# The closing rows of q's projection from VectorE's sums, q's modulated weights a tile later, and another order at the start

## The chip, the cores and the metric

The kernel runs on one core of one Trainium2 chip. The metric is the device time of one execution in microseconds (us), here the median of three runs. Beside it stands one execution recorded by the hardware profiler. The engines of the core are TensorE (PE; its weight loads are PEld), VectorE (DVE), ScalarE (ACT), GpSimd (POOL) and SyncE (SP, which only issues DMAs here). Each takes its instructions in the order of the program and waits for others through semaphores.

## What is computed

One block with adaptive layer norm (adaLN) over x of 2048 tokens by 448 channels, in fp32: a linear attention with 16 heads of 28 channels, then a token-mixing MLP with 1792 hidden units.

```python
mod = (silu(c) @ w_mod).reshape(1, 6, 1, 448)
sa, ca, ga, sb, cb, gb = [mod[:, i] for i in range(6)]
h = layernorm(x) * (1 + ca) + sa
x = x + ga * A(h, wqkv, wo)
h = layernorm(x) * (1 + cb) + sb
x = x + gb * B(h, w1, b1, w2, b2)

# A: q, k, v = split(h @ wqkv); phi(t) = where(t > 0, t + 1, exp(t)) + 1e-6
# kv = phi(k)^T v; z = sum over tokens of phi(k)
# o = phi(q) kv / (phi(q) . z + 1e-6); A = o @ wo
# B: transpose(gelu(w1^T h + b1) ...) over the token axis, @ w2 + b2
```

The first layer norm never appears as a tensor. With mean m and standard deviation s of a token, (LN(x) * (1 + ca) + sa) @ W equals (x @ W' - m * colsum(W') + s * (sa @ W)) / s, where W' is W with its rows scaled by 1 + ca. So x^T is multiplied by the modulated weight W', and two rows close the product: the negated column sums of W' (which meet the mean) and sa @ W (which meets the standard deviation). 1/s is applied as the scale of the activation that reads the result.

## The kernel before

All work is written out in program order by hand (`manual_schedule`): each engine executes its instructions in the order in which the code emits them. Tokens are worked in 16 tiles of 128. To keep fp32 precision with the faster fp32r matmuls, each operand is split into a rounded part ("high", made by a ScalarE copy) and the remainder ("low", a VectorE subtraction), and a product takes three matmuls: high by high, high by low, low by high. The 448 channels are four chunks: three of 128 and one of 64, whose upper half holds low parts.

**Buffers.** Most tiles come from a pool of 74 equal SBUF slots; PSUM is a pool of 8 banks of 128 by 512 (`bank`). A new tile waits until a buffer is free.

**Start (lines 88 to 219, 554 to 669).** Constants are made on POOL and VectorE, among them `mask` (a block diagonal of the heads, three POOL instructions; it is read only at line 806, after the kv loop) and the selectors `sel_f` and `sel_b`, whose columns 64, 66 and 96, and 65, 67 and 97, pick the closing rows. SP issues the loads. `col_sum(j, ch)` computes the columns 1 + ca (j = 1) and sa (j = 0) on VectorE. Index j of the weights is 0 for q, 1 for k, 2 for v. `w_high` (ScalarE) and `w_low` (VectorE) make the two parts of W'. `row_part(j, ch)` sums sa * W over the chunks on VectorE into `accb`. `row_sum(j)` multiplies the four high and three low parts by `sel_s` (seven fp32r matmuls); `row_bias(j)` adds the sums of `accb` by one fp32 matmul, which the profile shows as two steps. `row_out(j)` copies the rows out of PSUM (ScalarE) and makes their low part (VectorE) into `Wrow`. `close(t, j)` is the last matmul of each projection; it multiplies those rows by the transposed statistics of the tile.

**Statistics.** Tiles 0 and 1: `a_stats_act` on ScalarE, whose `end01` finishes on VectorE and POOL (`a_pow`, a power for standard deviation and its reciprocal). All others, in pairs: `a_stats_dve` on VectorE, with `first` (bn_stats), `second` (bn_aggr) and `end` (one VectorE step, then POOL's power). `a_rows(t)` spreads the statistics of a pair into a row tile, `a_transpose(t)` transposes it on TensorE into a bank, and `a_copy(t)`, `a_copy(t + 1)` bring it into the tiles' operands on ScalarE; `close` needs them.

**The kv loop (lines 672 to 762), t = 4 to 15.** In tile t TensorE gets, in this order: `project(t + 1, 1)` (ten matmuls of k), `close(t, 1)`, at t = 9 q's `row_sum(0)` and `row_bias(0)`, `a_outer(t - 4)` (eleven matmuls that add x^T phi(k) of tile t - 4 into the four `cacc` banks), at odd t a transpose of rows for tiles t + 1 and t + 2, from t = 10 one early projection of q (`a_q`, ten matmuls and a close), and at t = 12 `mod_sum2(2)`, one matmul into a bank that `mod_out(2)` empties. ScalarE gets the copies of rows, `a_exp` (exp and ReLU for phi(k), which free the bank of k's projection), the high parts for tile t + 3 (`a_split_high`), for phi(k) (`a_pk_parts`) and for the normed x of tile t - 2 (`a_high`), and at t = 4 to 7 `w_high(0, t - 4)`. VectorE gets the statistics of later tiles, `w_low` and `row_part` for q at t = 5 to 8, `a_norm`, `a_pk`, the low parts (`a_split_low`, `a_low`) and the sums of later modulations (`mod_part`). POOL issues accumulating DMAs (`pkl`, lines 521 and 535) and does the powers. `a_phi_q(keep)` runs exp, ReLU and phi on the q projections in PSUM but the last `keep`.

At t = 9 `a_exp(t, kp)` stands ahead of the two `a_copy`; at other tiles behind them. Q's early projections are those of tiles 0 to 4, at t = 10 to 14; the other eleven (`late`) follow behind the loop, where TensorE goes on with the last `a_outer`, kv, the output projection and the two matmuls of the MLP until the end.

Of the kernel before, what the change touches and what calls it, by code (L numbers as in the profile page):

```python
# [14 lines left out]
P = 128  # L15
# [9 lines left out]
PRE_LOAD = {14: 2, 15: 4}  # L25
KV_LAG = 4
HIGH_AT = {13: (11, 12), 14: (13,), 15: (14, 15)}
Q_EARLY = {10: 0, 11: 1, 12: 2, 13: 3, 14: 4}
RING = 3
FETCH = {4: 11, 5: 12, 7: 13, 9: 14, 10: 15}  # L30
SUM_DMA = range(2, 13)
# [21 lines left out]
def block_kernel(ctx: ExitStack, tc: tile.TileContext, x, xt, wqkv, wo, w1, b1, w2, b2, c, wmod, wfirst, out):  # L53
# [38 lines left out]
    ident = cst.tile([P, P], F32, name="ident")  # L92
    make_identity(nc, ident)
    mask = cst.tile([G, D], F32, name="mask")
    nc.gpsimd.memset(mask, 1.0)
    m3 = mask.rearrange("p (g h d) -> p g h d", g=4, d=DH)
    nc.gpsimd.affine_select(out=m3, in_=m3, compare_op=ALU.is_ge, fill=0.0, base=0,
                            pattern=[[0, 4], [-DH, 4], [0, DH]], channel_multiplier=1)
    nc.gpsimd.affine_select(out=m3, in_=m3, compare_op=ALU.is_ge, fill=0.0, base=DH - 1,
                            pattern=[[0, 4], [DH, 4], [0, DH]], channel_multiplier=-1)  # L100
# [10 lines left out]
    for i in (64, 66, 96):  # L111
        nc.gpsimd.memset(sel_f[:, i:i + 1], -1.0)
        nc.gpsimd.memset(sel_b[:, i + 1:i + 2], 1.0)
    sel_s = cst.tile([P, ROWS], F32R, name="sel_s")
    rowst = []
    for i in range(RING):
        rowst.append(cst.tile([P, P], F32R, name=f"rowst{i}"))
# [161 lines left out]
    def row_part(j, ch):  # L279
        if ch == 0:  # L280
            accb[j] = slot(f"accb{j}")
            nc.vector.tensor_scalar_mul(accb[j], raw_w[j, 0], col[0][:, 0:1])
        else:
            nc.vector.scalar_tensor_tensor(accb[j], raw_w[j, ch], col[0][:, ch:ch + 1], accb[j],
                                           op0=ALU.mult, op1=ALU.add)
# [6 lines left out]

    def row_bias(j):
        nc.tensor.matmul(rowb[j][:ROWS, :D], sel_b, accb.pop(j), start=False, stop=True)

    def row_out(j):
        ps, w = rowb.pop(j), Wrow[j]
# [284 lines left out]
    w_row(1)  # L582
    act01, end01 = a_stats_act((0, 1))
    act01(0)
    for ch in (0, 2):
        col_sum(0, ch)
        col_sum(0, ch + 1)
        row_part(1, ch)
        row_part(1, ch + 1)
    row_sum(1)  # L590
    act01(1)
    end01()
    a_split(3)
    projects(in_turn(3)[:4], 1, "kp")
    row_bias(1)
    projects(in_turn(3)[4:], 1, "kp")
    a_split_high(4)
    a_split_high(5)
    low = a_rows(0)
    first23, second23, end23 = a_stats_dve((2, 3))  # L600
    first23(0)
    low()
    first23(1)
    second23(0)
    second23(1)
    end23()
    row_out(1)
    a_split_low(4)
    a_transpose(0)
    a_copy(0)  # L610
    a_copy(1)
    a_norm(0)
    a_split_low(5)
    projects(in_turn(4)[:3], 1, "kp")
    kps = [close(t, 1) for t in (0, 1)]
    projects(in_turn(4)[3:], 1, "kp")
    load_xt(9)
    load_x(9)
    load_mod(2)
# [48 lines left out]
    sum_end()  # L668
    a_split(7)
    wo_sb = []  # L670
    late = [t for t in range(NT) if t not in Q_EARLY.values()]
    for t in range(4, NT):
        if 5 < t < NT - 1:
            project(t + 1, 1, "kp")
        kp = close(t, 1) if t > 4 else kps[4]
        if t == 9:
            row_sum(0)
            row_bias(0)
        if t > 4:
            a_outer(t - KV_LAG)  # L680
        if t % 2 and 4 < t < NT - 2:
            a_transpose(t + 1)
        if t in Q_EARLY:
            a_q(Q_EARLY[t])
        if t == 12:
            mp = mod_sum2(2)
        pair = t % 2 and 7 < t + 3 < NT
        if pair:
            first, second, end = a_stats_dve((t + 3, t + 4))
            first(0)  # L690
        if 5 <= t < 9:
            w_low(0, t - 5)
        if pair:
            second(0)
        if 5 <= t < 9:
            row_part(0, t - 5)
        a_phi_q(t in Q_EARLY)
        if t == 9:
            a_exp(t, kp)
        if t % 2 and 4 < t < NT - 2:  # L700
            a_copy(t + 1)
            a_copy(t + 2)
        if t != 9:
            a_exp(t, kp)
        if 7 < t + 3 < NT:
            a_split_high(t + 3)
        a_pk_parts(t - 1)
# [19 lines left out]
            second(1)  # L727
            end()
        sum_end()
        if 4 <= t < 8:  # L730
            w_high(0, t - 4)
            if t == 7:
                w_row(0)
        if t == 9:
            row_out(0)
        if t == 12:
            mod_out(2, mp)
        if t in FETCH:
            load_xt(FETCH[t])
            load_x(FETCH[t])  # L740
# [620 lines left out]
```

## Time and profile before

| | us |
|---|---|
| median of the three runs | 436.14 (436.09 to 436.59) |
| profiled execution, span | 434.3 |
| PE busy | 428.0 |
| DVE busy | 362.4 |
| ACT busy | 278.7 |
| POOL busy | 118.6 |

The views used below are: the chain of work that ended last (followed back from the last instruction, each step to what released it); windows (busy time of each engine in a stretch, with instruction counts, granted TensorE clock, DMA share and GB/s); and the timeline of one engine, where a row is start, duration, engine, line of the kernel, operation, output <- inputs, shapes and count, and in brackets the idle time before it with what ended it. Neighbours on VectorE and ScalarE overlap a little, so a step from start to start is shorter than the duration shown. Matmuls are pipelined: one of 448 columns shows 0.36 us but the next starts 0.20 us later.

### The profile page before, as it was taken

Reading aid. Unit: us, or ns where it says so; the run is one execution under the profiler, and the core shown is the slowest. Engines: PE = TensorE matmul, PEld = TensorE weight load, DVE = VectorE, ACT = ScalarE, POOL = GpSimd, SP = SyncE. Lnnn points to the kernel's source line nnn. Section 1 sums busy time; section 2 is a strip of 40 time slices with the busy share of each in tenths; the row PEclk is TensorE's granted clock in tenths of the full one; section 3 lists DMA queues with packets and bytes.
Section 4 is the critical chain, followed back from the end, with each engine's and each line's share of the span. In section 5 each row is a group of like instructions: output and inputs, shape, how many; then the busy total and the mean of one; then the engine's idle time right before and its main releaser. Section 6 shows DMA issues by size and latency. Waiting matters only on the chain.

```text
span 434.3 us, 7208 instructions
## 1 busy us (share of the span) xinstructions
PE 428.0 (99%) x2333; PEld 395.3 (91%) x2333; DVE 362.4 (83%) x813; ACT 278.7 (64%) x595; POOL 118.6 (27%) x198
## 2 busy tenths in 40 slices
PE   8999999999999999999999999999999999999996
PEld 7688899999799989989999999999999999999996
DVE  4899987689799999996679695739798998898893
ACT  5799868658568799985855273537464664645550
POOL 4335443200025477765200000010113131132010
PEclk9999999999999999999999999999999999999999
DMA  8998996564300036345427461587469987885430
GB/s 285 383 331 166 241 248 160 108 222 167 87 1 0 26 72 149 73 97 122 146 85 230 154 211 50 163 211 203 84 183 213 205 181 153 215 183 118 82 54 32
DMA packets 63941, 66.14 MB, mean 152 GB/s; under 512 B 4960, under 2 KB 55456, under 8 KB 63904
## 3 DMA queue, kind: packets, MB, share of 16 engines
q1 hardware_dynamic: 54832, 50.90, 37.5%
q0 software_dynamic: 8784, 14.32, 20.9%
q10 hardware_dynamic: 288, 0.46, 0.4%
q8 instruction: 18, 0.29, 0.3%
q14 instruction: 19, 0.16, 0.1%
HBM read 46.30 MB, written 7.34 MB: 124 GB/s over the span
## 4 chain that ended last, share of the span: by engine, by line
PE 92%; DVE 4%; DMA 2%; issue 1%; POOL 0%; ACT 0%; SPq 0%; DVEq 0%
PE y L1156 19%; PE up L935 10%; PE up L937 10%; PE up L936 10%; PE y L1157 9%; PE cacc L548 8%; PE qp L436 7%; PE op L878 6%; PE kp L436 5%; PE tq L848 1%; PE op L885 1%; DMA wr<-in_qkv_dram 1%; PE kp L443 1%; DMA xt<-in_xt_dram 1%; PE qp L443 1%; PE kvb L802 1%
## 5 line engine op out<-in xcount | busy, mean ns | idle before, releaser
L935 PE MATMUL up<-h2h,ph 128*128 128x448 f32 x224 | 81.3, 363 | 0.0
L937 PE MATMUL up<-h2h,pl 128*128 128x448 f32 x224 | 81.2, 362 | 0.0
L936 PE MATMUL up<-h2l,ph 128*128 128x448 f32 x224 | 80.8, 361 | 0.0
L1111 POOL DMA_DIRECT2D a<-a x16 | 14.1, 953 | 138.7 <-DMA a<-in_B_w_dram 77.5
L937 PEld LDWEIGHTS up<-h2h,pl 128*128 128x128 f32 x224 | 42.0, 188 | 3.2
L936 PEld LDWEIGHTS up<-h2l,ph 128*128 128x128 f32 x224 | 41.9, 187 | 3.2 <-DVE h2l L932 0.3
L935 PEld LDWEIGHTS up<-h2h,ph 128*128 128x128 f32 x224 | 42.0, 188 | 2.2
L85 DVE TENSOR_TENSOR pl<-pr,ph 128x512 fp32r<-128x512 f32 x46 | 30.8, 687 | 4.1 <-ACT ph L84 3.3
L1162 ACT ACTIVATE cc<-y 128x448 f32<-128x448 f32 x24 | 13.0, 545 | 26.9 <-PE y L1157 26.9
L84 ACT ACTIVATE ph<-pr 128x512 fp32r<-128x512 f32 x46 | 27.6, 622 | 0.8 <-PE up L937 0.5
L1075 DVE TENSOR_TENSOR u<-u,mod 128x448 f32<-128x448 f32 x14 | 8.7, 622 | 21.7 <-ACT u L1074 21.5
L1074 ACT ACTIVATE u<-up,b1c 128x448 f32<-128x448 f32 x14 | 8.7, 624 | 24.1 <-PE up L937 23.5
L436 PE MATMUL kp<-wh,hh 128*128 128x448 f32 x64 | 24.0, 380 | 0.0
L548 PE MATMUL cacc<-pkh,xh 128*128 128x448 f32 x64 | 23.6, 369 | 0.0
L1176 POOL DMA_DIRECT2D out_dram<-yt x14 | 12.7, 908 | 39.9 <-DVE yt L1167 30.6
L436 PE MATMUL qp<-wh,hh 128*128 128x448 f32 x64 | 23.4, 366 | 0.0
L828 POOL TENSOR_SCALAR den<-den 128x16 f32<-128x16 f32 x16 | 8.8, 548 | 45.3 <-DVE den L825 45.3
L548 PE MATMUL cacc<-pkl,xh 128*128 128x448 f32 x56 | 20.3, 362 | 0.0
L878 PE MATMUL op<-wph,pth 128*128 128x448 f32 x48 | 18.7, 389 | 0.0
L1117 DVE TENSOR_TENSOR a<-a,s 128x512 f32<-128x512 f32 (+1 forms) x32 | 18.5, 619 | 0.0
L84 ACT ACTIVATE s2h<-s 128x512 fp32r<-128x512 f32 (+1 forms) x16 | 8.3, 569 | 15.5 <-DVE s L1117 15.5
L1156 PE MATMUL y<-ub,a11h 128*128 128x448 f32 x56 | 18.2, 375 | 0.0
(239 smaller groups left out, 1376.4 us busy)
## 6 DMA issues: line engine op xcount, KB each, us to landing
pr<-in_B_w_dram SPq DMA_DIRECT2D x56, 256.0 KB, 3.0
a<-in_B_w_dram SPq DMA_DIRECT2D x32, 256.0 KB, 4.5
a<-in_B_w_dram SPq DMA_DIRECT2D x32, 192.0 KB, 4.5
xt<-in_xt_dram SPq DMA_DIRECT2D x16, 256.0 KB, 5.0
x<-in_A_x_dram SPq DMA_DIRECT2D x16, 224.0 KB, 5.0
wm<-in_B_wmod_dram SPq DMA_DIRECT2D x16, 196.0 KB, 5.0
out_dram<-x SPq DMA_DIRECT2D x14, 224.0 KB, 2.2
out_dram<-yt POOLq DMA_DIRECT2D x14, 224.0 KB, 5.4
```

The lines of the kernel that those rows point to most:

```text
L84: nc.scalar.activation(hi, full, AF.Copy)
L85: nc.vector.tensor_sub(lo, full, hi.bitcast(F32))
L436: nc.tensor.matmul(pps[t, j][:, :D], a[:, ch * P:(ch + 1) * P], w, start=first, stop=False)
L548: nc.tensor.matmul(cacc[ch][:, :D], a[:, s], b, start=(t == 0 and i == 0), stop=(t == NT - 1 and i == len(todo) - 1))
L878: nc.tensor.matmul(opb[t][:, :D], a, b, start=(ch == n == 0), stop=False)
L935: nc.tensor.matmul(ps[:, :D], hi[:, sl], mh, start=first, stop=False)
L936: nc.tensor.matmul(ps[:, :D], hi[:, sl], ml, start=False, stop=False)
L937: nc.tensor.matmul(ps[:, :D], lo[:, sl], mh, start=False, stop=last)
L1111: nc.gpsimd.dma_start(w, a, accum_op=ALU.add)
L1117: nc.vector.tensor_tensor(w, raw2[q, a][i], raw2[q, b][i], op=op)
L1156: nc.tensor.matmul(ps[:, :D], h[:, s], w, start=opens and r == 0, stop=False, skip_group_check=True)
L1157: nc.tensor.matmul(ps[:, :HD], l[:, s], wh, start=False, stop=closes and r == PAIRS - 1, skip_group_check=True)
```

## The change

Five edits. (1) The closing rows of q: VectorE sums (1 + ca) * W over the chunks (`row_main`, tiles 6 to 9) beside `row_part`'s sum; `row_fold` (tile 10) folds each 128-partition sum to 64 partitions in one tile, both sums together, and splits it into high and low; `row_both` (tile 11) multiplies them by a new selector `sel_q`, in two fp32r matmuls in place of seven and one. `sel_g` is filled by seven POOL memsets at the end of tile 7 and copied to `sel_q` on ScalarE. (2) `w_high`, `w_low` and `row_part` of q come a tile later. (3) Q's early projections move from tiles 10 to 14 to tiles 12 (two), 13, 14 and 15, and the special order at t = 9 goes. (4) At the start the statistics of tiles 0 and 1, their rows, the transpose, `row_out(1)` and the first two closes stand in another order. (5) `mask` is made at the end of tile 12.

```diff
-Q_EARLY = {10: 0, 11: 1, 12: 2, 13: 3, 14: 4}
+Q_EARLY = {12: (0, 1), 13: (2,), 14: (3,), 15: (4,)}
+ROW_AT, QPREP = 11, 5
...
-    nc.gpsimd.memset(mask, 1.0)
...
+    def make_mask():
+        nc.gpsimd.memset(mask, 1.0)
...
+    sel_g = cst.tile([P, ROWS], F32, name="sel_g")
+    sel_q = cst.tile([P, ROWS], F32R, name="sel_q")
...
+    accs = {}
+
+    def row_main(j, ch):
+        p = slice(0, P) if ch < 3 else slice(0, 64)
+        if ch == 0:
+            accs[j] = slot(f"accs{j}")
+            nc.vector.tensor_scalar_mul(accs[j], raw_w[j, 0], col[1][:, 0:1])
+        else:
+            nc.vector.scalar_tensor_tensor(accs[j][p], raw_w[j, ch][p], col[1][p, ch:ch + 1], accs[j][p],
+                                           op0=ALU.mult, op1=ALU.add)
+
+    def row_fold(j):
+        s, b = accs.pop(j), accb.pop(j)
+        nc.vector.tensor_add(s[:64], s[:64], s[64:])
+        nc.vector.tensor_add(s[64:], b[64:], b[:64])
+        hi, lo = moving(slot, f"rfh{j}"), moving(slot, f"rfl{j}")
+        nc.scalar.activation(hi, s, AF.Copy)
+        nc.vector.tensor_sub(lo, s, hi.bitcast(F32))
+        accs[j] = (hi, lo)
+
+    def row_both(j):
+        rowb[j] = bank(f"rowb{j}")
+        for i, m in enumerate(accs.pop(j)):
+            nc.tensor.matmul(rowb[j][:ROWS, :D], sel_q, m, start=(i == 0), stop=(i == 1))
...
     act01(0)
+    act01(1)
     for ch in (0, 2):
         col_sum(0, ch)
         col_sum(0, ch + 1)
+        if ch == 2:
+            end01()
         row_part(1, ch)
         row_part(1, ch + 1)
     row_sum(1)
-    act01(1)
-    end01()
+    a_rows(0)()
     a_split(3)
     projects(in_turn(3)[:4], 1, "kp")
     row_bias(1)
+    a_transpose(0)
     projects(in_turn(3)[4:], 1, "kp")
     a_split_high(4)
-    a_split_high(5)
-    low = a_rows(0)
     first23, second23, end23 = a_stats_dve((2, 3))
     first23(0)
-    low()
+    row_out(1)
+    a_copy(0)
+    a_copy(1)
+    a_split_high(5)
     first23(1)
     second23(0)
     second23(1)
     end23()
-    row_out(1)
+    kps = [close(t, 1) for t in (0, 1)]
     a_split_low(4)
-    a_transpose(0)
-    a_copy(0)
-    a_copy(1)
     a_norm(0)
     a_split_low(5)
-    projects(in_turn(4)[:3], 1, "kp")
-    kps = [close(t, 1) for t in (0, 1)]
-    projects(in_turn(4)[3:], 1, "kp")
+    projects(in_turn(4), 1, "kp")
...
-        if t == 9:
-            row_sum(0)
-            row_bias(0)
+        if t == ROW_AT:
+            row_both(0)
         if t > 4:
             a_outer(t - KV_LAG)
         if t % 2 and 4 < t < NT - 2:
             a_transpose(t + 1)
-        if t in Q_EARLY:
-            a_q(Q_EARLY[t])
+        for i in Q_EARLY.get(t, ()):
+            a_q(i)
...
-        if 5 <= t < 9:
-            w_low(0, t - 5)
+        if QPREP < t <= QPREP + 4:
+            w_low(0, t - QPREP - 1)
         if pair:
             second(0)
-        if 5 <= t < 9:
-            row_part(0, t - 5)
-        a_phi_q(t in Q_EARLY)
-        if t == 9:
-            a_exp(t, kp)
+        if QPREP < t <= QPREP + 4:
+            row_part(0, t - QPREP - 1)
+        if ROW_AT - 5 <= t < ROW_AT - 1:
+            row_main(0, t - ROW_AT + 5)
+        if t == ROW_AT - 1:
+            row_fold(0)
+        a_phi_q(len(Q_EARLY.get(t, ())))
         if t % 2 and 4 < t < NT - 2:
             a_copy(t + 1)
             a_copy(t + 2)
-        if t != 9:
-            a_exp(t, kp)
+        a_exp(t, kp)
...
-        if 4 <= t < 8:
-            w_high(0, t - 4)
-            if t == 7:
+        if QPREP <= t < QPREP + 4:
+            w_high(0, t - QPREP)
+            if t == QPREP + 3:
                 w_row(0)
-        if t == 9:
+        if t == 7:
+            nc.gpsimd.memset(sel_g, 0.0)
+            for i in (64, 66, 96):
+                nc.gpsimd.memset(sel_g[:64, i:i + 1], -1.0)
+                nc.gpsimd.memset(sel_g[64:, i + 1:i + 2], 1.0)
+            nc.scalar.activation(sel_q, sel_g, AF.Copy)
+        if t == ROW_AT:
             row_out(0)
         if t == 12:
             mod_out(2, mp)
+            make_mask()
```

More of the change, by code (lines that the diff above doesn't have):

```diff
@@ L94, in block_kernel @@
     mask = cst.tile([G, D], F32, name="mask")
[L95 to L100, printed above, removed]
+    def make_mask():
+        nc.gpsimd.memset(mask, 1.0)
+        m3 = mask.rearrange("p (g h d) -> p g h d", g=4, d=DH)
+        nc.gpsimd.affine_select(out=m3, in_=m3, compare_op=ALU.is_ge, fill=0.0, base=0,
+                                pattern=[[0, 4], [-DH, 4], [0, DH]], channel_multiplier=1)
+        nc.gpsimd.affine_select(out=m3, in_=m3, compare_op=ALU.is_ge, fill=0.0, base=DH - 1,
+                                pattern=[[0, 4], [DH, 4], [0, DH]], channel_multiplier=-1)
     cst.tile([P, 112], F32, name="space")
@@ L670, in block_kernel @@
     wo_sb = []
-    late = [t for t in range(NT) if t not in Q_EARLY.values()]
+    late = [t for t in range(NT) if t not in sum(Q_EARLY.values(), ())]
     for t in range(4, NT):
```

## The prediction

> **What bounds the kernel now.** I read first the chain of work that ended last, by engine, then the busy times of two stretches: tiles 4 to 9 of the kv loop (33 to 53.5 us) and its rest.
>
> ```profile
> PE 92%; DVE 4%; DMA 2%; issue 1%; POOL 0%; ACT 0%; SPq 0%; DVEq 0%
> ```
> ```profile
> 33.07:53.52 20.45, 20.45 (x100) 17.87 (x100) 20.05 (x51) 18.05 (x36) 11.43 (x12) 1.00 0.96 206
> 53.52:87.37 33.85, 33.85 (x170) 31.48 (x170) 25.35 (x60) 24.49 (x50) 11.48 (x12) 1.00 0.75 170
> ```
>
> The columns are the stretch, its length, then PE, PEld, DVE, ACT and POOL busy. TensorE bounds the whole: a matmul less is time gained, if nothing else then comes late. But in the first stretch VectorE is busy 20.05 of 20.45 us. It is a second bound there, with no room. After 53.5 us it has room (25.35 of 33.85), because TensorE is then given q's early projections (one a tile from tile 10). The profiled span is 434.3 us, 1.84 under the median of 436.14; I sum on the trace and add the result to the median.
>
> **The change part by part.**
>
> *The closing row of Wq on TensorE.* The chain has:
>
> ```profile
> 49.02 1.42 PE rowb L291 x7
> 50.44 0.75 PE rowb L294 x2
> ...
> 98.38 0.40 PE zp L781 x2
> ```
>
> Nine steps, 2.17 us, become two matmuls of the kind of L781, 0.40: **-1.8 us**.
>
> *The start.* Statistics of tiles 0 and 1 are finished earlier, and row_out(1) is moved ahead on VectorE.
>
> ```profile
> 15.22 0.19 ACT L344 ACTIVATION_READ_ACCUMULATOR junk<-x,as 128x1 f32 x1
> ...
> 15.51 1.39 DVE L284 SCALAR_TENSOR_TENSOR accb<-wr,col,accb 128x448 f32<-128x448 f32 x2
> 16.89 0.16 DVE L371 TENSOR_SCALAR ve<-as 128x4 f32<-128x4 f32 x1
> ...
> 17.13 1.41 POOL L356 TENSOR_TENSOR mv<-ve,roots 128x4 f32<-128x4 f32 x1 [3.76 <-DVE ve L371]
> ...
> 18.58 0.17 DVE L399 CAST rowst<-mv 128x8 fp32r<-128x8 f32 x1 [0.93 <-POOL mv L356]
> ...
> 20.33 0.63 DVE L299 TENSOR_TENSOR wrow<-rowb,wrow 2x448 fp32r<-2x448 f32 x1
> ...
> 21.11 0.65 PE L443 MATMUL kp<-wrow,hl 98*128 98x448 f32 x2 [0.76 <-DVE wrow L299]
> ```
>
> The sums of squares are there at 15.41, so `end01` can run between the two row pairs, at 15.51, instead of behind them near 16.9; POOL's power starts some 1.3 us earlier and VectorE's wait of 0.93 us shrinks to 0.2 or 0.3. TensorE's closing matmuls can start some 1.6 us earlier, but three matmuls that stood ahead of them now stand behind, and what follows waits for VectorE, which is nearly full from here on:
>
> ```profile
> 20.00:25.00 5.00, 4.24 (x21) 3.47 (x20) 4.87 (x13) 4.15 (x11) 1.01 (x1) 1.00 1.06 383
> ```
>
> So the gain is what VectorE's wait loses: **-0.7 us** on both engines.
>
> *The mask.* It leaves POOL's start, where the rows below give 1.91 us from its first step to `sel_b`; nobody waits for these. At tile 12 POOL is idle most of the time, and the mask is read only after the loop. Zero; with no such room it would delay the DMAs behind it by these 1.9 us.
>
> ```profile
> 1.32 0.47 POOL L95 MEMSET mask<- 112x448 f32 x1
> ...
> 3.23 0.20 POOL L108 MEMSET sel_b<- 128x98 f32 x1
> ```
>
> *What VectorE gets.* `row_main` is four more instructions of the kind of L282 and L284, `row_fold` two adds and a subtraction with a ScalarE copy in between, as in `halves` (L235, L240).
>
> ```profile
> 35.87 0.42 DVE L282 TENSOR_SCALAR accb<-wr,col 128x448 f32<-128x448 f32 x1
> ...
> 39.34 0.68 DVE L276 SCALAR_TENSOR_TENSOR wl<-wr,col,wh 128x448 fp32r<-128x448 f32 x1
> 39.94 0.68 DVE L284 SCALAR_TENSOR_TENSOR accb<-wr,col,accb 128x448 f32<-128x448 f32 x1
> ...
> 69.58 0.62 DVE L235 TENSOR_TENSOR acc<-acc 48x448 f32<-48x448 f32 x1
> 70.85 0.62 DVE L240 TENSOR_TENSOR mh<-acc,mh 64x448 fp32r<-64x448 f32 x1 [0.64 <-ACT mh L237]
> ```
>
> The long ones follow each other at 0.60 (39.34 to 39.94), overlapping by 0.08; the first row part takes 0.34 so reckoned. The fold costs 71.47 - 69.58 = 1.9 and another add of 0.54: 2.4 us. Together 0.34 + 3 x 0.60 + 2.4 = 4.5 us, all ahead of `row_both`, in the stretch where VectorE has 0.4 us free. `w_low` and `row_part` move from tiles 5 to 8 to tiles 6 to 9, so VectorE is 0.94 us ahead after tile 5, then pays +0.1, +0.6, +0.6 and +1.8 in tiles 6 to 9. [...]
>
> *A new wait on ScalarE.* The copy of `sel_g` into `sel_q` stands at the end of tile 7 in ScalarE's queue. It waits for POOL's memsets, which stand behind that tile's power and a DMA issue, and the power waits for VectorE's last statistics of the tile. Behind the copy stand exp(8) and all of tile 8, for which VectorE waits in turn.
>
> ```profile
> 47.69 0.17 DVE L390 TENSOR_SCALAR ve<-mv 128x4 f32<-128x4 f32 x1
> ...
> 48.25 0.69 DVE L276 SCALAR_TENSOR_TENSOR wh<-wr,col,wh 64x448 fp32r<-64x448 f32 x1
> ...
> 50.07 0.62 DVE L458 SCALAR_TENSOR_TENSOR pk<-ek,rk 128x448 f32<-128x448 f32 x1
> ...
> 51.28 0.22 DVE L505 TENSOR_TENSOR xh<-xn,xh 128x64 fp32r<-128x64 f32 x1
> ...
> 52.47 0.62 DVE L384 BATCH_NORM_STATS2 st<-x 128x6 f32<-128x448 f32 x1
> ```
> ```profile
> 47.95 1.17 POOL L356 TENSOR_TENSOR mv<-ve,roots 128x4 f32<-128x4 f32 x1 [0.67 <-DVE ve L390]
> 49.08 1.08 POOL L535 DMA_DIRECT2D pk<-pk  x1
> ```
> ```profile
> 3.87 0.29 ACT L556 ACTIVATE sel_s<-sel_f 128x98 fp32r<-128x98 f32 x1 [1.20 <-POOL sel_f L112]
> ...
> 47.49 0.62 ACT L450 ACTIVATE ek<-kp,mv 128x448 f32<-128x448 f32 x1
> ...
> 50.12 0.56 ACT L500 ACTIVATE xh<-xn 128x448 fp32r<-128x448 f32 x1
> ```
>
> VectorE's tile 8 starts at 48.25 now; in the new order at 48.25 - 0.7 - 0.94 + 0.1 + 0.6 = 47.3, and I take 47.8, half a microsecond for small waits (tile 9 has two, quoted below). The last statistics of tile 7 are then at 47.2, the power runs at 47.5 to 48.6, the DMA issue to 49.7, the seven memsets (the first 0.20 as L108, the others smaller) to 50.1, the copy (0.29 as L556) to 50.4, exp(8) and its ReLU, some 1.1, to 51.5. VectorE wants pk(8) at 47.8 + 1.82 + 0.60 = 50.2: it waits 1.4. The next, xh(6), ends 3.2 us behind exp(8)'s start (47.49 to 50.68), at 53.6, where VectorE comes at 51.6 + 1.2 = 52.8: it waits 0.85. Bounds of this part: zero, if POOL comes to the memsets early, and 2.25; I take **2.25**, since each link is in the rows. [...]
>
> *When `row_both` can run.* Tile 9 on VectorE now:
>
> ```profile
> 54.81 0.69 DVE L419 TENSOR_TENSOR hl<-xt,hh 128x512 fp32r<-128x512 f32 x1 [0.56 <-ACT hh L415]
> ...
> 56.36 0.23 DVE L505 TENSOR_TENSOR xh<-xn,xh 128x64 fp32r<-128x64 f32 x1 [0.32 <-ACT xh L500]
> ...
> 57.38 0.63 DVE L299 TENSOR_TENSOR wrow<-rowb,wrow 2x448 fp32r<-2x448 f32 x1
> ...
> 59.01 0.51 DVE L496 TENSOR_SCALAR xn<-x,mv 128x448 f32<-128x448 f32 x1
> ```
> ```profile
> 62.20 0.36 PE L548 MATMUL cacc<-pkh,xh 128*128 128x448 f32 x1
> ```
>
> Tile 9 starts at 47.8 + 4.22 + 0.60 + 2.25 = 54.9. It takes 6.54 now (52.47 to 59.01); without the two waits (1.0 with the lost overlaps) and row_out's 0.66 it is 4.85, with three added steps of 0.60 6.6: tile 10 starts at 61.5, the fold ends at 63.9, TensorE's `outer(7)` starts at **64.1**. `outer(7)` starts at 62.20 now, behind one q projection of eleven matmuls, 2.2 us at the 0.20 of L781's row. Without it, without the 2.2 of the row's nine steps and 0.7 earlier, TensorE would be at `row_both`, right ahead of `outer(7)`, at 57.1. It waits, first for hl(12) in tile 9 and then for the fold, and the new order still has that q projection ahead of it. So the net so far, with all gains of TensorE in it, is 64.1 + 2.2 - 62.2 = **+4.1 us**.
>
> *PSUM.* All eight banks count. At tile 11 the four `cacc`, kp11, kp12, `rowb` and the transposed rows are eight; kp13 needs the bank that the copies of the rows free. Now tile 9 frees kp9 early, by exp(9) ahead of the copies; that is taken out and not put at tile 11. At tile 13 the four `cacc`, kp13, q0, q1 and `modp` are eight, and kp14 waits for `mod_out(2)`.
>
> ```profile
> 53.25 0.27 PE L408 MATMUL rw<-ident,rowst 128*98 128x128 f32 x1
> ```
> ```profile
> 53.55 0.57 ACT L411 ACTIVATE hl<-rw 34x128 fp32r<-34x128 f32 x2 [1.82 <-PE rw L408]
> ...
> 74.87 0.52 ACT L201 ACTIVATE mod<-modp 128x448 f32<-128x448 f32 x1
> ```
>
> The first costs 53.25 to 54.12, some 0.85; the second 0.52 and a hand-over of 0.3 as between these rows, 0.8. From zero to 1.65; I take **1.6**, as the counts leave no ninth bank.
>
> *The rest.* Two q projections at tile 12 and one in each of 13 to 15 cost TensorE what they cost before. Buffers of q's tiles and of Wq are held about two tiles longer. SP's loads already wait for such buffers:
>
> ```profile
> SPq L138 <- DVE accb L284: 2.4, 1, 2.4
> ```
>
> They will land later, but have a tile or more in hand: zero; with that gone, a wait like this row's 2.4.
>
> Sum: +4.1 + 1.6 = **+5.7 us**: 440.0 on the trace, **441.8** beside the median.
>
> **The rivals.** (a) *Faster.* The added steps fall into room that VectorE finds; then only -1.8 and -0.7 stay: 433.6. For it: the two waits in tile 9. Against: they total 0.9 us in the rows, where 4.5 are added. The place is the end of the fold: if it comes before 58.2 on the trace (59.8 if no bank is short), the change gains, later it loses; I reckon 63.9. 13%. (b) *ScalarE's new wait costs nothing*: 2.25 less and 0.6 of the small waits, 439.0. 18%. (c) *A bank is free*: 440.2. 11%; (b) and (c) together 437.4, 5%. (d) *The clock falls while TensorE waits* about 2.4 us at `row_both`. The granted clock is 1.00 in the stretches above and TensorE's longest wait in these rows is 0.76, so none shows it. At half speed the 11 + 10 matmuls behind, of 0.2 each, would take 4.2 us more: 446.0. 4%. [...] (e) *Nothing*: the VectorE load is half of what I reckon and eats the gains, 436.1. 3%.
>
> **How the numbers follow.** The forecast has 46%, with 440.4 to 443.2 as its own range (the 0.5 of small waits, a power of 1.17 or 1.41, one bank wait less or smaller). Leaving out (a), (d) and (e) is 20%, so the range reaches from (b) with (c) to the forecast's upper end: 437.2 to 443.2. About 0.2%, 0.9 us, is what can be told from no change. Faster 13%; same 5%, (e) and some of (b) with (c); slower 82%.
>
> **What would show it.** Right: ScalarE idle some 4 us ahead of the copy to `sel_q`, released by POOL; VectorE waiting at pk(8); VectorE full from 34 to 64 us; TensorE waiting about 2 us or more at `row_both` for the fold; gaps of 0.8 ahead of kp13 and kp14; the start 0.7 earlier. Wrong: TensorE without gaps from 50 to 64 us, or a fold that ends before 60.

## The result, and the profile after

| | before | after |
|---|---|---|
| median of the timed runs, us | 436.12 (435.98 to 436.59) | 447.27 (446.91 to 447.74) |
| profiled execution, span | 434.3 | 445.2 |
| mean granted TensorE clock | 1.000 | 0.991 |
| TensorE's row matmul `zp` (the landmark ahead of the kv product) starts at | 98.21 | 107.96 |

The changed kernel takes 11.15 us more: a ratio of 1.0257 (1.0244 to 1.0269). 441.8 was forecast with a range up to 443.2, so the sign was right and the size was not. Of the 10.9 us between the two traces 9.8 are there when `zp` starts; the kv loop is the place.

The chain of work that ended last, after, by engine:

```profile
PE 83%; DVE 8%; ACT 3%; DMA 2%; POOL 1%; issue 1%; SPq 0%; DVEq 0%; ACTq 0%; POOLq 0%
```

TensorE had 92% of it before. The missing part went to VectorE, ScalarE and POOL. TensorE's own waits name the places (engine, line waited for: us in total, times, longest):

```profile
PE rw L439 <- DVE rowst L433: 4.2, 2, 4.0
PE rowb L325 <- ACT rfh L318: 2.2, 1, 2.2
PE warm L192 <- DVE roots L110: 1.1, 1, 1.1
PE kp L467 <- ACT hl L442: 0.7, 1, 0.7
PE kp L467 <- ACT mod L207: 0.6, 1, 0.6
```

The two largest are new: 4.0 us at a transpose of rows, 2.2 at `row_both`. The two of 0.7 and 0.6 stand ahead of the projections of tiles 13 and 14. The 4.0 is read backwards through three queues. First TensorE and VectorE:

```profile
50.04 0.37 PE L579 MATMUL cacc<-pkl,xh 128*128 128x448 f32 x1
54.42 0.32 PE L439 MATMUL rw<-ident,rowst 128*98 128x128 f32 x1 [4.02 <-DVE rowst L433]
```
```profile
50.42 0.17 DVE L430 CAST rowst<-mv 128x8 fp32r<-128x8 f32 x1 [0.50 <-POOL mv L387]
53.67 0.63 DVE L489 SCALAR_TENSOR_TENSOR pk<-ek,rk 128x448 f32<-128x448 f32 x1 [3.07 <-ACT rk L484]
54.21 0.16 DVE L433 TENSOR_TENSOR rowst<-mv,rowst 128x4 fp32r<-128x4 f32 x1
...
55.73 0.23 DVE L536 TENSOR_TENSOR xh<-xn,xh 128x64 fp32r<-128x64 f32 x1 [0.76 <-ACT xh L531]
```

The step that TensorE wants, L433, takes 0.16 us and its inputs had been there since 50.6. It stands behind phi(k) (L489) in VectorE's queue, and that waits 3.07 us for ScalarE's ReLU. Now ScalarE and POOL:

```profile
45.30 0.66 ACT L270 ACTIVATE wh<-wr,col 128x448 fp32r<-128x448 f32 x1
52.30 0.28 ACT L769 ACTIVATE sel_q<-sel_g 128x98 fp32r<-128x98 f32 x1 [6.35 <-POOL sel_g L768]
52.49 0.62 ACT L481 ACTIVATE ek<-kp,mv 128x448 f32<-128x448 f32 x1
53.01 0.62 ACT L484 ACTIVATE rk<-kp,mv 128x448 f32<-128x448 f32 x1
```
```profile
47.43 2.96 POOL L387 TENSOR_TENSOR mv<-ve,roots 128x4 f32<-128x4 f32 x1 [1.25 <-DVE ve L421]
50.36 0.91 POOL L566 DMA_DIRECT2D pk<-pk  x1
50.97 0.50 POOL L765 MEMSET sel_g<- 128x98 f32 x1
```

ScalarE stands idle for 6.35 us ahead of a copy of 0.28; some 2.2 of these it would have waited in any case, as k's projection of tile 8, which exp(8) behind the copy needs, ends at 48.2. The memsets that it waits for start at 50.97, behind a power that takes 2.96 us here (1.17 before) and a DMA issue; the first takes 0.50, the last ends at 52.26.

What the long wait does to TensorE's clock is in windows (stretch, length, PE busy, granted clock, DMA share, GB/s):

```profile
50.00:55.00 5.00, 0.98 (x5) 1.00 0.95 220
55.00:60.00 5.00, 5.00 (x18) 0.66 0.70 138
60.00:65.00 5.00, 3.34 (x16) 1.00 0.58 130
65.00:70.00 5.00, 4.47 (x14) 0.66 0.61 146
70.00:75.00 5.00, 4.34 (x22) 1.00 1.03 247
```

In 55 to 60 us TensorE is never idle and gets through 18 matmuls; 25 fit in at 0.20 a step. Its steps are 0.37 us from 55.0 to 58.7, and most of them again from 65.5 to 68.9, behind the wait at `row_both`. The wait of 4.0 and the first of these stretches cost nothing by themselves: between 55.7 us and the fold VectorE waits for nobody, and TensorE comes early enough to stand 2.2 us for the fold all the same. What sets the time here is how late the fold is.

### The profile page after: what moved, and what is told of

It is laid out like the page before. It is cut to its first block, busy times and chain, and to the rows that moved or that the text cites. A ratio compares the mean times of both kernels' runs of the same rounds, so it can differ in the third digit from the quotient of the medians.

```text
span 445.2 us, 7207 instructions
## 1 busy us (share of the span) xinstructions
PE 432.1 (97%) x2326; PEld 396.2 (89%) x2326; DVE 367.3 (82%) x820; ACT 279.7 (63%) x597; POOL 121.0 (27%) x205
## 2 busy tenths in 40 slices
DMA packets 63941, 66.14 MB, mean 149 GB/s; under 512 B 4960, under 2 KB 55456, under 8 KB 63904
## 4 chain that ended last, share of the span: by engine, by line
PE 83%; DVE 8%; ACT 3%; DMA 2%; POOL 1%; issue 1%; SPq 0%; DVEq 0%; ACTq 0%; POOLq 0%
PE y L1193 18%; PE up L972 10%; PE up L974 10%; PE up L973 10%; PE y L1194 9%; PE qp L467 7%; PE op L915 7%; PE cacc L579 4%; PE kp L467 1%; PE tq L885 1%; PE op L922 1%; DVE st L415 1%; DMA wr<-in_qkv_dram 1%; DVE hl L450 1%; POOL mv L387 1%
## 5 line engine op out<-in xcount | busy, mean ns | idle before, releaser
L467 PE MATMUL kp<-wl,hh 128*128 128x448 f32 x48 | 18.0, 382 | 0.4 <-DVE wl L282 0.4
L1193 PE MATMUL y<-ub,a12h 128*128 128x448 f32 x56 | 18.3, 376 | 0.0
```

Source lines behind the costliest of these rows:

```text
L1193: nc.tensor.matmul(ps[:, :D], h[:, s], w, start=opens and r == 0, stop=False, skip_group_check=True)
```

## The experiments

Each kernel was timed against the kernel before, in the same session; "above before" is the difference of the two medians.

**The copy alone.** The first run makes the selector at the start, all else as changed (e1).

```diff
+    nc.gpsimd.memset(sel_g, 0.0)
...
     nc.scalar.activation(sel_s, sel_f, AF.Copy)
+    nc.scalar.activation(sel_q, sel_g, AF.Copy)
...
-        if t == 7:
-            nc.gpsimd.memset(sel_g, 0.0)
...
-            nc.scalar.activation(sel_q, sel_g, AF.Copy)
```

> The changed kernel, but sel_g is filled and copied to sel_q at the start, beside sel_s. Theory (ScalarE's wait for POOL at tile 7 is the largest loss): ScalarE's 6.3 us wait, VectorE's 3.1 at pk(8) and TensorE's 4.0 at the rows of tile 10 go, the fold ends near 62.0 instead of 66.1, and the clock no longer falls at tile 10: about 442.0. Rival (VectorE's sums fill the stretch by themselves): 446 to 447. Rival (late loads hold it): 446 to 447, with the wait for x at tile 10 still there.

Measured: 443.18, ratio 1.0172 (1.0154 to 1.0190), 7.1 above before. The place of the copy costs **4.1 us**. In the traces, which both have their first closing matmul at 19.60, `row_both` starts at 61.52 in place of 65.53. TensorE's wait at the row transposes goes from 4.2 to 1.1 us; the wait at `row_both` stays at 2.2.

The opposite test puts the memsets and the copy into the kernel before, where nobody reads `sel_q` (e5).

```diff
+        if t == 7:
+            nc.gpsimd.memset(sel_g, 0.0)
...
+            nc.scalar.activation(sel_q, sel_g, AF.Copy)
         if t == 9:
             row_out(0)
```

> The kernel before, with nothing but sel_g and its copy to sel_q at the end of tile 7 added (nothing reads them). Theory: ScalarE waits some 4 us for POOL, VectorE 2 to 3 us at pk(8), and since the rows of tile 10 had only 2.5 us in hand, TensorE waits some 1 us: 437 to 437.5. With this little of a wait the clock stays at 1.00. Rival (the wait costs its whole length wherever it stands): 439 to 440. Rival (it costs only beside the sums): 436.1.

Measured: 440.87, ratio 1.0107 (1.0088 to 1.0126), 4.8 above before. In the trace of this run:

```profile
51.16 0.29 ACT L741 ACTIVATE sel_q<-sel_g 128x98 fp32r<-128x98 f32 x1 [3.65 <-POOL sel_g L740]
```
```profile
53.38 0.29 PE L410 MATMUL rw<-ident,rowst 128*98 128x128 f32 x1
55.66 0.47 PE L438 MATMUL kp<-wh,hh 128*128 128x448 f32 x1 [1.99 <-ACT rk L455]
```

ScalarE waits 3.65 us and TensorE 1.99, here for a PSUM bank that the late exp and ReLU free. This trace is 2.7 us late at `zp` (100.87 against 98.21) and 3.8 at its end; the other 1.2 come where TensorE has no wait at all. That remainder led to the places of the buffers, below. The median lies 1.0 above this execution: in two of the four the granted clock was lower (441.47 and 441.53 us at a mean of 0.995, against 439.82 at 0.998).

**The PSUM releases.** e1, with exp and ReLU of tile 11 ahead of the copies of the rows and `mod_sum2(2)` with `mod_out(2)` at tile 13 (e2).

```diff
+            if t == ROW_AT:
+                a_exp(t, kp)
             a_copy(t + 1)
             a_copy(t + 2)
-        a_exp(t, kp)
+        if t != ROW_AT:
+            a_exp(t, kp)
...
-        if t == 12:
+        if t == 13:
             mp = mod_sum2(2)
```

> As e1_sel_early, and the two waits for a PSUM bank taken away: exp(11) ahead of the copies of rows, the sum of modulation 2 and its copy at tile 13. Theory: the gaps of 0.66 and 0.63 ahead of the projections of tiles 13 and 14 go, 1.3 under e1_sel_early, about 440.7. Rival (those gaps only move to the next wait): within 0.4 of e1_sel_early.

Measured: 441.59, ratio 1.0128 (1.0114 to 1.0142): **1.6 us** less than e1. The gap ahead of tile 14's projection is gone; that ahead of tile 13's stays at 0.7 and is now released by the ReLU. So the 1.6 is not the two releases alone. In e1's trace 3.4 us at half clock begin at `row_both`, in e2's none do, and from `row_both` to the close of tile 13's projection of k it is 7.8 us (61.52 to 69.33) in e1 and 6.3 (62.21 to 68.50) in e2.

**The parts that were costed at little or nothing.** The start order on the kernel before (e3), the mask at tile 12 on the kernel before (e6), and both (e11).

```diff
+        if ch == 2:
+            end01()
...
-    act01(1)
-    end01()
+    a_rows(0)()
```

> The kernel before with the new order at the start alone. Theory: VectorE's and TensorE's start is 0.5 to 0.7 us earlier and nothing gives it back: 435.4 to 435.6. Rival (VectorE's full stretch of tiles 4 to 9 takes it back): 436.1.

> The kernel before, with the mask made at the end of tile 12 alone. Theory: nothing waits for it, 436.1 within 0.4. Rival (POOL's three instructions at tile 12 delay the DMAs behind them): up to 2 us more.

> The kernel before with the new order of the first tiles and the mask at tile 12, without VectorE's sums and without q's weights a tile later; no tile is added. Each alone gave 435.72 and 435.96. Theory: together 435.6, at most 0.5 below before; rival: 436.0, no difference.

Measured: e3 435.72, ratio 0.9993 (0.9984 to 1.0002); e6 435.96, 0.9997 (0.9988 to 1.0006); both 435.79, 0.9995 (0.9987 to 1.0004). None can be told from the kernel before. The mask is free. The start order gains 0.35 us by the medians, with an interval from 0.7 less to 0.1 more; the closing matmuls start earlier, but at tile 4 of the loop the traces differ by 0.1 (30.04 before, 29.95 in e3), and at `zp` by 0.2.

**Without VectorE's sums.** The changed kernel with the old seven matmuls and the bias matmul at tile 11 in place of sums and selectors (e4); the same with e2's releases (e4b).

```diff
-            row_both(0)
+            row_sum(0)
+            row_bias(0)
...
-        if ROW_AT - 5 <= t < ROW_AT - 1:
-            row_main(0, t - ROW_AT + 5)
-        if t == ROW_AT - 1:
-            row_fold(0)
```

> The changed kernel without VectorE's sums and the new selectors: q's closing rows by the seven and one matmuls of before, at tile 11; q's weights a tile later and q's projections at tiles 12 to 15 as in the change. Theory: TensorE has no q projection to fill tiles 10 and 11 and the two bank waits stay, but VectorE is not overfilled: about 438.4. Rival (the sums are the whole loss): 435.5 to 436. Rival (moving the projections is the whole loss): 442 or more.

> e4_no_sums with the two waits for a bank taken away as in e2_sel_early_banks. It differs from e2_sel_early_banks only by VectorE's sums and the closing rows. Theory: the gaps of 0.65 and 2.0 go, and what is left is TensorE's two tiles without a q projection: 437 to 439, so the sums cost 2.5 to 4.5 of what e2_sel_early_banks has. Rival (the gaps move to the next wait): 441 or more, and the sums cost nothing.

Measured: e4 442.69, ratio 1.0154 (1.0135 to 1.0172), scattered from 441.45 to 444.04; e4b 444.06, 1.0178 (1.0161 to 1.0195), worse, though it was to be better. ScalarE's waits in e4b say why:

```profile
ACT ek L481 <- DMA pk<-pk: 7.0, 1, 7.0
```

The exp of tile 11, put first in ScalarE's queue, needs a buffer that an accumulating DMA still holds, and everything behind it waits 7.0 us. In e4 the same wait is 2.3. The likely reason is that weights and projections of q, held a tile or two longer, leave too few of the 74 buffers; no run with more buffers was made. So these two kernels don't measure the sums by themselves, and how the loss divides between the sums and the moved projections of q stays open.

Everything of q one tile earlier, the early projections spread over tiles 11 to 15, on e2 (e7):

```diff
-Q_EARLY = {12: (0, 1), 13: (2,), 14: (3,), 15: (4,)}
-ROW_AT, QPREP = 11, 5
+Q_EARLY = {11: (0,), 12: (1,), 13: (2,), 14: (3,), 15: (4,)}
+ROW_AT, QPREP = 10, 4
```

> e2_sel_early_banks with q's weights at the tiles of before (high parts at 4 to 7, low parts, row parts and sums at 5 to 8), the fold at tile 9, the closing rows at tile 10 and one q projection in each of tiles 11 to 15. Theory (VectorE's sums are late for TensorE because no projection covers them): less TensorE waiting at the closing rows, 437 to 438.5, still above before. Rival (the sums cost the same wherever they stand): 441 to 442. POOL's power at the end of tile 7 takes near 3 us again if three VectorE instructions with two inputs behind each other hold it up.

Measured: 441.57, ratio 1.0123 (1.0108 to 1.0138), the same as e2. The wait at `row_both` gives way to one of 2.25 at the close of a projection: the copy of the rows that it needs stands in ScalarE's queue behind the high part of the fold, which waits 3.95 us there for VectorE's sums.

**The places of the buffers.** Behind the loop, the eleven matmuls of a q projection take longer after the change. The first rows are of before, the second of after, start to start:

```profile
131.12 0.36 PE L436 MATMUL qp<-wh,hh 128*128 128x448 f32 x1
...
133.32 0.36 PE L885 MATMUL op<-wph,pth 128*128 128x448 f32 x1
```
```profile
141.17 0.36 PE L467 MATMUL qp<-wh,hh 128*128 128x448 f32 x1
...
143.42 0.37 PE L922 MATMUL op<-wph,pth 128*128 128x448 f32 x1
```

2.20 against 2.25 us, 0.200 and 0.2045 a step, with no wait among them and the granted clock at 1.00. All runs with the tiles `sel_g` and `sel_q` showed the long step, e3 and e6 the short one. So the kernel before was run with nothing but a wider unused tile (e8).

```diff
-    cst.tile([P, 112], F32, name="space")
+    cst.tile([P, 308], F32, name="space")
```

> The kernel before with its tile space 196 columns wider (112 to 308): the 784 bytes that sel_g and sel_q of 98 columns each add to the constants in the changed kernel, and nothing else. Nothing reads or writes that tile. In all runs with sel_g and sel_q (the changed kernel and the runs with the sums or with the copy alone) ten matmuls and the row matmul of a q projection take 2.24 to 2.25 us behind the kv loop, in those without (before, start order alone, mask alone) 2.20. Theory A: it is where the buffers lie; then this kernel shows 2.24 too, with no wait in it, and takes 1.1 to 2.3 us more: 437.2 to 438.4. Theory B: it follows the long wait of TensorE in the loop, or the work itself; then 2.20 and 436.1.

Measured: 438.03, ratio 1.0050 (1.0037 to 1.0063), **2.1 us** above before. No instruction differs and TensorE has no wait in the kv loop in either, but the steps are long:

```profile
131.98 0.37 PE L436 MATMUL qp<-wh,hh 128*128 128x448 f32 x1
...
134.24 0.37 PE L885 MATMUL op<-wph,pth 128*128 128x448 f32 x1
```

Five runs then tried to put the buffers back, by a shift of about 2048 bytes (e9 on the changed kernel, e10 on e2), and by making room for `sel_q` in the tile `space` while `sel_g` takes `sel_f`'s memory (e12 on the changed kernel, e13 on e5; e14 on e2, where POOL writes `sel_q` at once and `sel_g` and the copy are gone). e15 is e4 without the two tiles.

```diff
-    cst.tile([P, 112], F32, name="space")
+    cst.tile([P, 14], F32, name="space")
...
-    sel_g = cst.tile([P, ROWS], F32, name="sel_g")
+    sel_g = sel_f
```

> The changed kernel with its tile space 316 columns wider (112 to 428), so that sel_g, sel_q and the wider tile together move the later buffers by 2048 bytes, the size of one slot. Theory A (where the buffers lie): the q projections take 2.20 us again and the kernel 445.0 to 446.2. Theory B (the wait or the work): 2.24 and 447.3.

> The version with the copy at the start and the two PSUM releases mended (441.59), with the tile space 316 columns wider as in the run beside it. Theory A: 439.3 to 440.5, and the waits of TensorE that are left in it (row_both 2.4, row transposes 1.0, projections 1.4, less the 1.8 us of the closing row) then make up the whole of what it is above before. Theory B: 441.6.

> The changed kernel with the constants kept to the bytes they had before: sel_g takes sel_f's memory (sel_f has been copied to sel_s long before), and the tile space is 98 columns narrower (112 to 14), which makes room for sel_q. Every later buffer then lies where it lay before the change. Theory: the q projections take 2.20 us again and the kernel 2.1 us less than the changed one, 445.2; all waits of TensorE stay (4.2 at the row transposes, 2.2 at row_both). Rival, by which the places matter only in the kernel before: 447.3.

> The kernel before with the memsets and the copy at the end of tile 7, that nobody reads, and with all later buffers at the places of before (sel_g in sel_f's memory, space 14). Theory: of the 4.8 us of the run with the copy alone 2.1 were places and 2.7 the wait: 438.7. Rival, the whole 4.8 is the wait: 440.8.

> The version with the PSUM releases mended and the selector made at the start, here written by GpSimd into sel_q at once, without sel_g and without ScalarE's copy; space 14, so all later buffers lie as before. Theory: 441.5 less 2.1 is 439.4; what is left above before (3.4) are the waits at row_both (2.4), the row transposes (1.0) and the projections (1.4) less the closing row (1.8). Rival: 441.5, the places don't matter here.

> The run without VectorE's sums, without the two tiles sel_g and sel_q, which it doesn't use; all later buffers lie as before. Theory: 442.7 less 2.1 is 440.6, and the rest above before are waits for buffers and banks (2.0 and 0.7 in its trace). Rival: 442.7.

Measured: e9 447.31 (1.0259, 1.0245 to 1.0273), e10 441.33 (1.0121, 1.0106 to 1.0137), e12 447.51 (1.0264, 1.0250 to 1.0278), e13 442.06 (1.0130, 1.0116 to 1.0144), e14 442.27 (1.0142, 1.0129 to 1.0156): no gain, and long steps in all five. What the copy's wait alone costs at the old places was so not measured. e13 differs from e5 in the clock too: in its trace 3.4 us at half clock follow TensorE's wait of 2.0, and it is 4.5 us late at `zp` (102.72) where e5 is 2.7. e15 gave 440.98 (1.0119, 1.0098 to 1.0139), 1.7 less than e4, with short steps. The addresses in the built programs explain the misses: each tile is rounded up to 32 bytes. The shift was 2112 bytes in e9 and e10 and 32 in e12 to e14, not 2048 and 0. (By the same rounding the changed kernel's is 832 and e8's is 800.) With `space` at 8 columns the buffers behind the constants lie exactly as before (e16 on the changed kernel, e17 on e14).

```diff
-    cst.tile([P, 112], F32, name="space")
+    cst.tile([P, 8], F32, name="space")
```

> The changed kernel with sel_g in sel_f's memory and the tile space at 8 columns. The three runs before with space 14 were to leave all later buffers in place, but each tile starts at a multiple of 32 bytes: by the addresses in the built programs their tok buffers (the heads' and tokens' buffers, 2048 bytes each, that lie behind the constants) start at 168608, 32 bytes further than the 168576 of before; with 8 columns they start at 168576. By the programs, the starts of the slower runs are 169376 (only a wider tile), 169408 (changed), 170688, 168608, those of the runs at 0.200 to 0.202 a step all 168576. Theory: the steps are 0.200 again and the kernel takes 445.2 (2.1 less than the changed one, the 2.1 that the wider tile alone cost); waits of TensorE as in the changed kernel. Rival: it isn't the start of tok, 447.3.

> The version with the PSUM releases mended and sel_q written by GpSimd at the start, with the tile space at 8 columns: tok starts at 168576 as before. With 14 columns (start 168608) it took 442.27. Theory: 440.2, steps 0.200; what is left above before (4.1) is the waits of TensorE at row_both (2.4), the row transposes (1.0) and the projections (1.3), and what a lower clock behind them adds, less the closing row. Rival: 442.3.

Measured: e16 445.92 (444.36 to 445.99), ratio 1.0219 (1.0204 to 1.0233); e17 **439.94** (439.62 to 440.26), ratio 1.0091 (1.0077 to 1.0104). e17 is 2.3 below e14, which differs by 32 bytes; e16 is 1.4 below the changed kernel, and its steps are short too:

```profile
141.04 0.36 PE L467 MATMUL qp<-wh,hh 128*128 128x448 f32 x1
...
143.25 0.37 PE L922 MATMUL op<-wph,pth 128*128 128x448 f32 x1
```

It isn't a full 2.1 below. From `zp` to the end it is 1.2 faster (336.0 us against 337.2), and that is all that the changed kernel's places cost there. At `zp` it is 0.3 later (108.23), and it was 0.4 later already at the first closing matmul (20.01 against 19.60), well ahead of the copy; why is open. Its clock is lower in 55 to 60 us, 0.50 where the changed kernel had 0.66, but TensorE still waits 1.4 us for the fold behind that.

```profile
55.00:60.00 5.00, 5.00 (x15) 0.50 0.74 141
```

Taking the eighteen runs and the two kernels themselves, a q projection behind the loop takes 2.20 to 2.22 us in the seven whose `tok` buffers (the heads' and tokens' buffers behind the constants) start at byte 168576 and 2.24 to 2.26 in the thirteen with other starts (the fourth of the eleven takes 0.1 more in every kernel). The starts have an order that fits all twenty:

| start of `tok`, bytes | multiple of | q projection, us | `zp` to the end, us | kernels |
|---|---|---|---|---|
| 168576 | 128 | 2.20 to 2.22 | 336.0 to 336.1 | before, e3, e6, e11, e15, e16, e17 |
| 169408, 170688 | 64, not 128 | 2.24 to 2.26 | 337.2 to 337.3 | changed, e1, e2, e4, e4b, e5, e7, e9, e10 |
| 168608, 169376 | 32, not 64 | 2.26 | 337.7 | e8, e12, e13, e14 |

So e8, with a shift of 800 bytes, lies in a worse class than the changed kernel with 832: behind `zp` it loses 1.6, the changed kernel 1.2. The order was seen afterwards in five starts; no run was made to test it (another multiple of 128 would), nor was it tried which of the moved buffers matters.

**What is left.** TensorE's waits in e17, which has neither the copy's wait nor moved buffers:

```profile
PE rowb L328 <- ACT rfh L321: 2.2, 1, 2.2
PE warm L195 <- DVE roots L110: 1.1, 1, 1.1
PE rw L442 <- DVE rowst L436: 1.2, 2, 1.0
PE kp L470 <- ACT rk L487: 0.7, 1, 0.7
PE kp L470 <- DVE hl L453: 0.7, 1, 0.7
PE rowb L328 <- DVE rfl L322: 0.2, 1, 0.2
```

Those of the loop are 0.96, 0.68, 2.21, 0.21 and 0.74 at their rows, 4.80 in all. A wait costs TensorE more than the idle time shown, since that is counted from the end of the matmul before. In the changed kernel:

```profile
79.92 0.36 PE L263 MATMUL modp<-mh,ones_r 128*128 128x448 f32 x1
80.91 0.48 PE L467 MATMUL kp<-wh,hh 128*128 128x448 f32 x1 [0.63 <-ACT mod L207]
```

From start to start 0.99, and 0.32 to the matmul after it (81.23), in place of 0.20 each: 0.91 for an idle time of 0.63. With 0.28 more for each of the five the waits are an estimated 6.2 us; less the closing row (1.8) and the start (0.3) that is 4.1. Measured are 3.8 (439.94 less 436.10). No run separates these waits from each other.

## Why the prediction was right or wrong

The loss of 11.15 us comes apart along a chain of kernels: 4.1 for the copy's place (changed to e1), 1.6 for the releases and the clock that came with them (e1 to e2), 1.7 for the buffers' places (e2 to e17, which also leaves out the copy at the start; 1.4 from the changed kernel to e16), and 3.8 for what is left (e17 to before). The four add up because each kernel follows from the last; in another order the parts could differ.

*The closing row (-1.8)*: right as far as the runs go. Two matmuls stand in place of nine steps, and with -1.8 the sum of e17 closes to 0.3; no run has this part alone.

*The start (-0.7)*: not shown. Up to the closing matmuls it is early (19.60 against 21.11), but e3 gives 0.35, not to be told from none and just not excluding 0.7; its trace has 0.2 at `zp`.

*The mask (0)*: right (e6).

*VectorE's added steps (4.5)*: the duration was right. The fold's adds follow each other at 0.66 (63.59 and 64.25), without overlap, where the forecast put 0.54 on an add. The second add also overwrites what the first reads, so these two don't show why. A pair in the kernel before has no overlap either, without such a tie: `w_low` of the last chunk works on partitions 64 to 127 and ends at 48.94, and `row_part` behind it, which needs nothing of it, starts at 48.97; on all partitions the same pair overlaps by 0.08 (39.34 and 39.94). What takes the overlap away was not tested. TensorE waits 2.2 at `row_both` even where ScalarE's copy costs nothing (e2, e17); that is the part of the forecast in which the sums themselves are late. Rival (a), by which the sums find room, is refuted by e17: without the copy's wait and with the releases mended it is still slower than before.

*The new wait on ScalarE (2.25)*: **this is the step that failed, in its size.** The links were the right ones: power, DMA issue, memsets, copy, exp, phi(k). Their durations were not. The power took 2.96, not 1.17; the memsets 1.3 (50.97 to 52.26), not 0.4. The copy was ready at 52.58, not at 50.4, VectorE waited 3.07 at phi(k), not 1.4, and 0.76 at xh, not 0.85. (By the forecast's own times, 51.5 less 50.2 and 53.6 less 52.8, it had 1.3 and 0.8, 2.1 in all.) Without the copy there (e1) the fold starts at 59.58 and not at 63.59, so the term was 4.0, not 2.25. It made the fold end 2.2 us later than forecast (66.14, not 63.9); `outer(7)` started at 66.68, not 64.1. The 2.25 was taken as the upper bound of this part, but each link was priced by a row with other neighbours.

*The queue behind the waiting instruction* was followed to the fold only. The forecast has TensorE wait "first for hl(12) in tile 9 and then for the fold". The step of 0.16 us that makes the next rows for TensorE stands behind phi(k) as well, so TensorE stood for 4.0 us already at 50.4. This adds nothing to the time, since the fold comes later still; the first stretch of low clock follows it.

*The clock, rival (d)*: its mechanism came true, as an addition to the forecast and not in its place. It was priced at 4.2 us for 21 matmuls at half speed behind a wait of 2.4, and had 4%. In the trace the half clock lasts 3.4 us each time. The first stretch is covered by the wait for the fold. Of the second, six steps of `outer(7)` (66.68 to 68.92) take 0.37 in place of 0.20, which is 1.0 us. Which waits bring it can be read from the granted clock. In every trace its changes lie at whole multiples of 3.413 us from each other (55.28, 58.70, 65.52 and 68.94 in the changed kernel). Cut at these marks, here are two stretches of the changed kernel, then three of e2 (stretch, length, busy time and count of PE, PEld, DVE, ACT and POOL, granted clock, DMA share, GB/s):

```profile
62.11:65.52 3.41, 1.23 (x7) 0.79 (x5) 2.67 (x8) 0.62 (x2) 2.22 (x2) 1.00 0.96 224
65.52:68.94 3.42, 3.41 (x9) 2.69 (x10) 2.67 (x8) 3.03 (x6) 0.41 (x1) 0.50 0.72 169
```
```profile
57.90:61.32 3.42, 2.09 (x9) 1.61 (x9) 3.32 (x9) 0.00 (x0) 1.95 (x2) 1.00 0.74 161
61.32:64.73 3.41, 2.30 (x10) 1.92 (x11) 2.57 (x7) 3.12 (x7) 0.33 (x1) 1.00 0.87 224
64.73:68.14 3.41, 2.68 (x14) 2.17 (x14) 2.81 (x7) 3.30 (x9) 1.75 (x2) 1.00 0.58 145
```

The wait of 2.2 falls into one stretch in the changed kernel, where PE is busy 1.23 us and the clock halves behind it; in e2, and so in e17, it falls across two with 2.1 and 2.3, and nothing follows. In the twenty traces, from 15 to 430 us, each stretch at full clock with 1.80 us of PE or less (e16, 64.26 to 67.68) is followed by half clock, and none with 1.82 or more (e9, 64.95 to 68.36; 1.96 in the changed kernel, 48.45 to 51.87). The mean granted clock of one kernel differs from execution to execution (0.987 to 0.996 in e16). The author's estimate is that its waits lie differently on these marks, so the medians hold some luck. In e16 1.6 us of idle time in one stretch were enough, so the forecast's wait of 2.4 could bring the half clock where it fell into one.

*The PSUM releases (1.6)*: the two gaps came, 0.66 and 0.63 of idle time in the trace, near the 0.85 and 0.8 of the forecast once the lost overlap is counted. That e1 to e2 gives the same 1.6 is luck in part: the gap ahead of tile 13 didn't go away with its release, which was only one of the things it waited for, and the clock differs between the two traces.

*Late buffers (0)*: in the changed kernel nothing contradicts it. In e4 and e4b, which move q in the same way, it does not hold: ScalarE waits 2.3 and 7.0 us for a buffer.

*The places of the buffers* don't occur in the forecast. A term of nothing was so put on two more tiles of 98 columns; by their places they cost the changed kernel 1.2 us behind `zp` and 1.4 by the medians (e16).

By the forecast's own steps: the net with the late fold is 66.68 + 2.2 - 62.2 = +6.7 and not +4.1, the releases +1.6, the half clock in `outer(7)` +1.0, the longer steps behind `zp` +1.2: 10.5, where the traces differ by 10.9; 0.4 stays open.

The power's 2.96 us was not tested by itself. The traces have it beside one, two or three of VectorE's instructions with two tensors that follow without a gap:

```profile
47.62 0.68 DVE L282 SCALAR_TENSOR_TENSOR wl<-wr,col,wh 128x448 fp32r<-128x448 f32 x1
48.22 0.68 DVE L290 SCALAR_TENSOR_TENSOR accb<-wr,col,accb 128x448 f32<-128x448 f32 x1
48.81 0.68 DVE L310 SCALAR_TENSOR_TENSOR accs<-wr,col,accs 128x448 f32<-128x448 f32 x1
```

Behind these three in the changed kernel it ends at 50.39, 0.9 behind the last. In e4, with the first two alone, it takes 2.41; in the kernel before, where a gap of 0.03 follows the first, 1.17. The number of them alone doesn't decide: in e7 a power at 39.90 takes 1.40 beside three such instructions (39.72, 40.31 and 40.91), and in the kernel before one at 39.52 takes 1.56 beside two (39.34 and 39.94). There the first of them started 0.2 ahead of the power, in the long cases 0.2 behind it. The spans on POOL are rough in the profile, and no run changed the order or the number alone, so what makes the power long was not shown.

## What to carry to other kernels

Where an instruction is put into an engine's queue with a wait, follow every consumer of what stands behind it, down to the smallest: a step of 0.16 us held TensorE for 4.0, here hidden by a fold that was later still. Take the duration of the link that the wait depends on from rows with the new neighbours, not the old ones. And two runs with a changed kernel's allocations alone, the old ones and the new ones, tell whether a few hundred bytes of constants cost more than the instructions; compare addresses in the built program, since sizes are rounded up (here to 32 bytes). A wait can be paid twice, by its idle time and by a stretch of half clock (3.4 us each time in the changed kernel), and the granted clock differs from execution to execution (means of 0.987 to 0.996 in e16).

## What the runs showed of the hardware

- The same matmuls, with the same operands and no wait, take 2.20, 2.24 or 2.26 us per eleven depending on where the buffers lie; 32 bytes are enough (e14 to e17). The five starts order by whether they are multiples of 128, 64 or 32 bytes, which no run was made to test. From `zp` to the end that is 1.2 us, or 1.6 to 1.8.
- TensorE's granted clock changes on marks 3.413 us apart. In the twenty traces it halves for one such stretch or two behind a stretch with at most 1.80 us of busy PE (e16), and not behind 1.82 or more (e9).
- A power of 128 x 4 elements on POOL took 1.03 to 1.56 us at most places of the loop and 2.41 or 2.96 at others; VectorE's instructions beside it differ, but what decides was not tested.
- On POOL memsets of one column on 64 partitions took 0.13 us each from start to start, in tile 7 as at the start (e1), where those on 128 partitions took 0.03; the six of the changed kernel took 0.8, the forecast had 0.2. The first memset took 0.50 in tile 7 and 0.18 at the start (e1).
